# Row maxima of an attention block taken over every sixth query, and carried to their row by one transfer

## The chip, the cores and the metric

The kernel runs on one core of a Trainium2 chip. The metric is the device time of one execution in microseconds (us), the median of several. Matrix products run on TensorE (PE in the rows, with PEld for the loading of its weights), reductions on VectorE (DVE), exponentials and copies on ScalarE (ACT), some additions on GpSimd (POOL), and nearly all transfers are issued by SyncE (SP).

## The reference

Attention over 2 x 8 heads of 768 queries and keys with 64 values each, in which a query sees only the keys of its own cluster, and then two MLPs on the 1536 tokens. What the change touches is the maximum of each query's scores:

```
mask = q_assign[:, :, :, None] == k_assign[:, :, None, :]
scores = scale * np.matmul(q, k.transpose(0, 1, 3, 2))
scores = np.where(mask, scores, -1000000000.0)
scores = scores - np.max(scores, axis=-1, keepdims=True)
attn = np.exp(scores)
attn = attn / (np.sum(attn, axis=-1, keepdims=True) + 1e-09)
return np.matmul(attn, v).astype(np.float32)
```

## The kernel before

The 16 heads (h = 0 to 15) go one after the other through a software pipeline whose order is written out by hand, engine by engine. After it come the MLPs, whose order is set by a planner; the change doesn't touch them.

For each head, two tensors of 128 partitions hold what the products need: `q2(h)` and `k2(h)`, each with two layers of 768 columns. In layer 1, rows 0 to 63 are the queries (keys), rows 64 to 79 mark the cluster, and row 96 (`MROW`) of `q2` holds, for each of the 768 queries, the negative of its maximum. `k2` has ones in that row, so that the scores come out of TensorE with the maximum taken off.

The scores (`st`, line 707) are made with keys on the partitions: 12 steps per head (6 blocks of 128 keys by 2 halves of 384 queries), each of two matmuls: the first over layer 0, the second over rows 0 to 96 of layer 1, `MROW` among them. Beside each step of head h, one of the 12 matmuls `smax` (line 657) of head h + 1 runs: a block of 128 queries is the weight (80 rows by 128 columns), 384 keys are streamed, and VectorE takes the maximum of each query's 384 scores into `nm[:, c, n]` (line 662).

After the 12 steps, `mneg(h + 1)` (line 673) reduces the two halves to `nr`, 128 partitions by 6 numbers, with the sign turned. Block c holds the queries c*128 to c*128 + 127, so partition p of `nr` has the queries p, 128 + p, 256 + p and so on. To bring them into one row in order, `mrow` multiplies `nr` by the identity on TensorE (out: 6 partitions by 128), ScalarE copies the result from PSUM to `row`, and one transfer on SP sends its 6 pieces of 512 bytes to `MROW`. In the heads 2 to 14 the two products with the values of blocks 0 and 1 (`values(h, 0)`, `values(h, 1)`, line 739: `pv`) stand ahead of `mrow` on TensorE, and the rest of the values (`pv`, and the sums `ps`) behind it. The odd heads 5 to 11 have eight more matmuls (`sims`, line 572) between the last step and the values. Head 1 calls `mrow(2)` in another place, ahead of products of another kind (line 807). In all, `mrow` runs 14 times. The heads 0 and 1 get their maxima in another way (`mrow_at_once`), which stays.

The first matmul of head h + 1 that reads `MROW` is the second `st` of its first step, after all values of head h. The first `smax` beside it, of head h + 2, reads rows of `k2` that ScalarE has cast (line 642) in the even heads.

Of the kernel before, what the change touches and what calls it, by code (L numbers as in the profile page):

```python
# [8 lines left out]
F32 = mybir.dt.float32  # L9
F32R = mybir.dt.float32r  # L10
# [174 lines left out]
def tile_cluster_attention_two_mlps(ctx: ExitStack, tc: tile.TileContext, qk, v, cen, w1, w2, wg, wv, w3, out):  # L185
    nc = tc.nc
    B, H, D, _, S = qk.shape
    NC = cen.shape[0] // H
# [4 lines left out]
    SC = S // 128  # L193
# [26 lines left out]
    def take_bank(pl, tag, shape, name):  # L220

        if tag == "m":
            bank[0] ^= 1
            tag = f"m{bank[0]}"
        return pl.tile(shape, F32, tag=tag, name=name)
# [168 lines left out]
    sm_p = pool(att, "sm", 2)  # L394
    r_p.append(pool(att, "r1", 1))
    ps_x = pool(att, "ps_x", 1, space=PSUM)
# [20 lines left out]
    ONE, MROW = D, 96  # L417

    def q2(h):
        return q2_t[h % NQK]  # L420
# [140 lines left out]
    ident_r = acst.tile([128, 128], F32R, name="ident_r")  # L561

    def similar(hs, pl=ps_x, tag="x"):


        out = []
        for h in hs:
            ps = take_bank(pl, tag, [128, 512], "sims")[:, 0:HALF]
            todo = [(i, n) for i in (0, 1) for n in range(2)]
            for at, (i, n) in enumerate(todo):  # L570
                o = LEAD + 128 * (h % H) - 32 * (2 * n + i)
                nc.tensor.matmul(  # L572
                    out=ps,
                    lhsT=cs[:, i, o:o + 128],
                    rhs=(q2, k2)[i](h)[:, 0, n * HALF:(n + 1) * HALF],
                    start=(at == 0),
                    stop=(at == len(todo) - 1),
                )
            out.append(ps)
        return out  # L580
# [71 lines left out]
    def smax(h, c, n, pl, tag):  # L652

        if c == 0 and n == 0:
            nm_t[h] = sm_p.tile([128, SC, 2], F32, tag="nm", name="nm")
        ps = take_bank(pl, tag, [128, 512], "smax")[:, 0:HALF]
        nc.tensor.matmul(  # L657
            out=ps,
            lhsT=q2(h)[0:ONE + NC, 1, c * 128:(c + 1) * 128],
            rhs=k2(h)[0:ONE + NC, 1, n * HALF:(n + 1) * HALF],  # L660
        )
        nc.vector.tensor_reduce(out=nm_t[h][:, c, n:n + 1], in_=ps, axis=AX.X, op=ALU.max)  # L662
# [5 lines left out]
    nr_t = {}  # L668

    def mneg(h, cs=slice(None)):  # L670
        if h not in nr_t:
            nr_t[h] = sm_p.tile([128, SC], F32R, tag="nr", name="nr")
        nc.vector.tensor_reduce(out=nr_t[h][:, cs], in_=nm_t[h][:, cs, :], axis=AX.X, op=ALU.max, negate=True)
# [9 lines left out]
            )  # L683
        nc.scalar.copy(q2(h)[MROW:MROW + 1, 1, n * HALF:(n + 1) * HALF], ps)

    def mrow(h, pl=ps_x, tag="x"):

        ps = take_bank(pl, tag, [SC, 128], "mrow")
        nc.tensor.matmul(out=ps, lhsT=nr_t.pop(h), rhs=ident_r)  # L689
        row = sm_p.tile([SC, 128], F32R, tag="row", name="row")  # L690
        nc.scalar.copy(row, ps)
        nc.sync.dma_start(
            out=q2(h)[MROW:MROW + 1, 1, :].rearrange("p (c s) -> p c s", s=128).bitcast(F32), in_=row.bitcast(F32)
        )

    p_t = {}
# [307 lines left out]
    for h in range(NH):  # L1004
        more, ahead = h + 1 < NH, h + 4 < NH
        maxima = list(steps) if more and h > 1 else []
        for i, step in () if h in (0, NH - 1) else list(enumerate(steps))[2 * EARLY if h == 1 else 0:]:
            scores(h, *step)
            if maxima:
                next_smax(h + 1, maxima)  # L1010
            if h > 1:
                beside_scores(h, i)
            if h > 2 and i == 4:
                moved_sums(h - 1)
                send_sums(h - 1)
        if h == NH - 1:
            moved_sums(h - 1)
            send_sums(h - 1)
            load_sums((h - 3) // 2)
        elif h > 2:  # L1020
            moved(h - 1)
            if h % 2 and 4 < h < NH - 1:
                load_sums((h - 3) // 2)
        if h == 0:
            load_qk(5)
        if h == 1:
            do(assign([2, 3], (nc.vector.tensor_copy, nc.gpsimd.tensor_copy)))
            norm(0)
            lo_k(4, nc.gpsimd)
            lo_q(4, nc.gpsimd)  # L1030
        if h == 2:
            norm(1)
        if 1 < h < NH - 1:
            mneg(h + 1)
            if h % 2 and ahead and h > 3:
                do(largest([h + 3, h + 4], similar([h + 3, h + 4], ps_s, "s")))
            if h > 3 and h + 5 < NH:
                hi_staged(h + 5)
            values(h, 0)
            values(h, 1)  # L1040
            mrow(h + 1)
        casts = [] if not h else [h + 4] if h < 3 else [7, 8] if h == 3 else [h + 5] if h + 5 < NH else []
        if h > 3 and casts:
            hi_others(casts[0])
        elif casts and h != 1:
            hi_q(casts[0])
            hi_k(casts[0])
        elif casts:
            hi_q(casts[0])
        if h % 2 == 0 and 0 < h < NH - 3:  # L1050
            do(assign([h + 2, h + 3]))
        if NH - 4 <= h < NH - 1:
            close_slot(h % NQK)
        if h == NH - 4:
            w_p = right("w", WB - 1)
        if h == NH - 3:
            s_p.append(right("s", 1))
            b_p.update({i: right(f"b{i}", 1) for i in (1, 2)})
        if h == NH - 2:
            b_p[0] = right("b0", 1)  # L1060
            c_p.append(right("c", CB // 2))
            e_p.append(right("e", 1))
        for c in range(SC) if more else ():
            if h > 1:
                if c > 1:
                    values(h, c)
                beside_block(h, c)
            elif h or c:
                pv(h, c)
            if c == 0:  # L1070
                if h < 2:
                    load_v(h + 1)
                    if h:
                        load_v(h + 2)
                        hi_k(casts[0])
                    for i in casts:
                        lo_q(i, nc.gpsimd)
                        lo_k(i, nc.gpsimd)
                    load_qk(h + 6)
                if ahead:  # L1080
                    if h + 5 == NH:
                        close_slot(FIRST)
                        close_slot("st")
                        xs_p.append(right("xs", 2))
                        xc_p.append(right("xc1", XC - X0 - 1))
            if h == 0:
                beside(1, c, ((ps_m, "m"), (ps_s, "s")))
                if c == 2:
                    sims = similar([2])
                if c == 3:  # L1090
                    mneg(1)
                    mrow_at_once(1, 0, ps_o, "o")
                    mrow_at_once(1, 1, ps_m, "m")
                    sims += similar([3], ps_m, "m")
                    do(largest([2, 3], sims))
                if c in (3, 4):
                    for step in steps[EARLY * (c - 3):EARLY * (c - 2)]:
                        scores(1, *step)
            if h == 1:
                beside(2, c, ((ps_m, "m"), (ps_s, "s")))  # L1100
                if c == 3:
                    mneg(2)
                    sims = similar([4], ps_s, "s")
                    mrow(2)
                if c == 4:
                    do(largest([4, 5], sims + similar([5], ps_s, "s")))
            for i in casts[-1:] if h > 3 else ():
                for at, step in ((1, lo_staged), (2, spread_lo)):
                    if c == at:
                        step(i)  # L1110
            if h > 1 and c == 2:
                if h + 2 < NH:
                    load_v(h + 2)
                if h + 6 < NH:
                    load_qk(h + 6)
            for part in takes.get((h, c), ()):
                take(part)
            if h in (2, 3) and c == 1:
                lo_q(casts[0])
                lo_k(casts[0])  # L1120
            for n in beside_values.get((h, c), ()):
                next(more_steps[n], None)
            if h == 1 and c == 4:
                fetch_to(2)
            if h == 3 and c == 4:
                do(largest([6, 7], similar([6, 7], ps_s, "s")))
                hi_staged(8)
                hi_others(8)
            if h == 4 and c == 1:
                lo_staged(8)  # L1130
                spread_lo(8)
            if h == 3 and c in (3, 4):
                to_x(0, c - 3)
# [568 lines left out]
```

## Time and profile before

| | |
|---|---|
| median of 3 runs | 776.87 us (776.78 to 777.65) |
| profiled execution, own time | 778.64 us |
| its span | 776.9 us |
| TensorE busy in the span | 769.1 us (99%) |
| VectorE, ScalarE, GpSimd busy | 665.6, 504.6, 126.6 us |
| chain that ended last, TensorE's share | 92% |
| `mrow` matmuls (line 689) | 14 |
| `smax` matmuls (line 657), heads 0 to 15 | 192 |

A span is the time from the first to the last instruction of the profiled execution; 1.7 us lie around it. The busy time of TensorE is partly modelled, so that a busy TensorE can still lose time between two matmuls. The chain of work that ended last shows this better: it is followed back from the last instruction and gives each piece the time until the next one.

### The profile page before, as it was taken

The numbers are of one execution on the slowest core, as the hardware profiler recorded it, in microseconds if no ns is written. First come the engines' busy times: TensorE is split into PE (matmuls) and PEld (weight loads), VectorE is DVE, ScalarE is ACT, GpSimd is POOL, SyncE is SP. The second block draws the span as 40 slices with busy tenths as digits, with TensorE's granted clock in tenths as the row PEclk, the third lists the DMA queues.
The fourth block names the chain that finished last, engine by engine and source line by source line (L and its number), as shares of the span: only waits on it lengthen the run. The fifth ranks groups of instructions, "written<-read, shape, count | busy, mean of one in ns | idle before, by whom it ended". The sixth has DMA issues, their size and how long they took to land.

```text
span 776.9 us, 11963 instructions
## 1 busy us (share of the span) xinstructions
PE 769.1 (99%) x4238; PEld 662.6 (85%) x4238; DVE 665.6 (86%) x1220; ACT 504.6 (65%) x875; POOL 126.6 (16%) x136
## 2 busy tenths in 40 slices
PE   8999999999999999999999999999999999999998
PEld 6996676766767999999999999999999999999996
DVE  7887899998994999999798889999987997877752
ACT  7848988996866877777676677666544644443322
POOL 7655344453544000100000000000000000000000
PEclk9999999999999999999999999999999999999999
DMA  4231155643214686653186783657433122412102
GB/s 114 51 101 37 37 137 146 171 105 80 65 33 157 220 268 208 211 176 105 39 271 225 279 282 109 232 173 234 136 109 107 57 82 82 135 56 82 55 1 81
DMA packets 52507, 101.94 MB, mean 131 GB/s; under 512 B 19600, under 2 KB 25088, under 8 KB 52448
## 3 DMA queue, kind: packets, MB, share of 16 engines
q1 hardware_dynamic: 52224, 100.86, 41.5%
q8 instruction: 33, 0.54, 0.3%
q10 hardware_dynamic: 224, 0.33, 0.1%
q14 instruction: 26, 0.21, 0.1%
HBM read 76.23 MB, written 21.06 MB: 125 GB/s over the span
## 4 chain that ended last, share of the span: by engine, by line
PE 92%; DVE 5%; ACT 1%; issue 1%; POOL 1%; DMA 0%; POOLq 0%; DVEq 0%; ACTq 0%
PE h L384 36%; PE a L384 29%; PE st L707 8%; PE pv L739 7%; PE smax L657 4%; PE ps L739 3%; PE pv L807 2%; PE sims L572 2%; DVE nm L662 1%; PE warm L492 1%; DVE b L379 0%; DMA w<-scr 0%; DVE u L1301 0%; PE mrow L689 0%; DVE wo L291 0%
## 5 line engine op out<-in xcount | busy, mean ns | idle before, releaser
L384 PE MATMUL h<-xc,b 128*128 128x384 f32 x1680 | 317.0, 337 | 0.1
L384 PEld LDWEIGHTS h<-xc,b 128*128 128x128 f32 x1680 | 291.5, 188 | 10.6 <-DVE u L1301 2.4
L384 PE MATMUL a<-g,sp 128*128 128x512 f32 (+1 forms) x768 | 144.3, 337 | 0.0
L384 PEld LDWEIGHTS a<-g,sp 128*128 128x128 f32 x768 | 125.0, 188 | 16.8
L384 PE MATMUL a<-sp,g 128*128 128x512 f32 x432 | 109.6, 393 | 0.0
L726 POOL TENSOR_TENSOR add<-p 128x384 f32<-128x384 f32 x84 | 84.4, 1026 | 105.4 <-ACT p L717 104.4
L662 DVE TENSOR_REDUCE nm<-smax 128x1 f32<-128x384 f32 x192 | 97.6, 553 | 4.5 <-PE smax L657 4.0
L717 ACT ACTIVATE p<-st 128x384 f32<-128x384 f32 x192 | 87.9, 491 | 20.6 <-PE st L707 15.7
L707 PE MATMUL st<-q,k 128*128 128x384 f32 (+1 forms) x384 | 97.8, 345 | 0.1
L384 PEld LDWEIGHTS a<-sp,g 128*128 128x128 f32 x432 | 80.2, 188 | 13.2
L376 ACT CAST b<-s 128x512 fp32r<-128x512 f32 x80 | 49.5, 619 | 56.0 <-PE h L384 45.5
L707 PEld LDWEIGHTS st<-q,k 128*128 128x128 f32 (+1 forms) x384 | 68.2, 190 | 10.0 <-issue 7.2
L739 PE MATMUL pv<-p,v 128*64 128x384 f32 x336 | 65.2, 495 | 0.0
L657 PE MATMUL smax<-k,q 80*128 80x384 f32 x192 | 63.5, 348 | 1.1 <-DVE nm L662 0.9
L1301 DVE TENSOR_TENSOR u<-h,p 128x384 f32<-128x384 f32 x80 | 44.1, 552 | 21.9 <-PE h L384 21.6
L280 ACT ACTIVATE a<-raw 128x512 f32<-128x512 f32 x68 | 45.5, 670 | 19.5 <-issue 9.4
L379 DVE TENSOR_TENSOR b<-s,b 128x512 fp32r<-128x512 f32 x80 | 54.6, 684 | 1.6 <-ACT b L376 0.4
L379 DVE TENSOR_TENSOR g<-c,g 128x768 fp32r<-128x768 f32 x56 | 52.5, 951 | 1.6 <-ACT g L376 0.9
L376 ACT CAST g<-c 128x768 fp32r<-128x768 f32 x56 | 45.3, 835 | 12.3 <-DVE c L1316 11.8
L286 DVE SCALAR_TENSOR_TENSOR t<-a,t 128x512 int32<-128x512 int32 x68 | 46.0, 682 | 4.0 <-ACT t L283 4.0
L1309 ACT ACTIVATE c<-c 128x384 f32<-128x384 f32 (+1 forms) x56 | 38.3, 684 | 16.8 <-DVE c L1301 16.1
L376 ACT CAST b<-w 128x768 fp32r<-128x768 f32 x35 | 29.2, 834 | 29.2 <-PE h L384 28.8
(144 smaller groups left out, 904.6 us busy)
## 6 DMA issues: line engine op xcount, KB each, us to landing
raw<-in_w SPq DMA_DIRECT2D x44, 512.0 KB
w<-scr SPq DMA_DIRECT2D x30, 512.0 KB
raw<-in_wg SPq DMA_DIRECT2D x12, 512.0 KB
raw<-in_wv SPq DMA_DIRECT2D x12, 512.0 KB
w<-scrg SPq DMA_DIRECT2D x12, 512.0 KB
w<-scrv SPq DMA_DIRECT2D x12, 512.0 KB
st<-in_qk SPq DMA_DIRECT2D x31, 192.0 KB
scr<-wd SPq DMA_DIRECT2D x23, 256.0 KB
```

What stands on the lines that cost most here:

```text
L280: nc.scalar.activation(a, raw[:, :, 1].bitcast(F32), ACTF.Copy, scale=2.0**-112)
L286: nc.vector.scalar_tensor_tensor(out=t, in0=a.bitcast(I32), scalar=3, in1=t, op0=ALU.logical_shift_left, op1=ALU.bitwise_or)
L376: nc.scalar.copy(to, of)
L379: eng.tensor_tensor(out=to, in0=of, in1=hi.bitcast(F32), op=ALU.subtract)
L384: nc.tensor.matmul(out=out_ps, lhsT=lhs[a], rhs=rhs[b], start=(start and j == 0), stop=(stop and j == 2), skip_group_check=True, **kw)
L657: nc.tensor.matmul(out=ps, lhsT=q2(h)[0:ONE + NC, 1, c * 128:(c + 1) * 128], rhs=k2(h)[0:ONE + NC, 1, n * HALF:(n + 1) * HALF],)
L662: nc.vector.tensor_reduce(out=nm_t[h][:, c, n:n + 1], in_=ps, axis=AX.X, op=ALU.max)
L707: nc.tensor.matmul(out=ps, lhsT=k2(h)[0:rows, a, c * 128:(c + 1) * 128], rhs=q2(h)[0:rows, a, at], start=(a == 0), stop=(a == 1),)
L717: nc.scalar.activation(p_t[h, c][:, n * HALF:(n + 1) * HALF], ps, ACTF.Exp, scale=scale)
L726: nc.gpsimd.tensor_tensor(out=add_t[h, c][:, at], in0=p_t[h, c][:, at], in1=p_t[h, c + 1][:, at], op=ALU.add)
L739: nc.tensor.matmul(out=ps[n * D:(n + 1) * D, 0:HALF], lhsT=w, rhs=x[:, n * HALF:(n + 1) * HALF], start=start, stop=stop, skip_group_check= ...
L1301: lambda: nc.vector.tensor_tensor(out=to.tile[:, part], in0=ps.tile[:, 0:HALF], in1=other.tile, op=ALU.add),
```

## The change

In the heads 2 to 15, block c of `smax` takes the queries c, c + 6, c + 12 and so on (`c::SC`, SC is 6): the 128 columns of the weight then lie 24 bytes apart, where they were side by side. Partition p of `nr` so holds the six queries 6p to 6p + 5, which are neighbours in `MROW`. The matmul by the identity, the copy from PSUM and the tile `row` are gone; `mrow` is one transfer from `nr` itself, 128 pieces of 24 bytes. The call of `mrow` moves up behind `mneg`.

```
@@ smax
-            lhsT=q2(h)[0:ONE + NC, 1, c * 128:(c + 1) * 128],
+            lhsT=q2(h)[0:ONE + NC, 1, c::SC] if h > 1 else q2(h)[0:ONE + NC, 1, c * 128:(c + 1) * 128],
@@ mrow
-    def mrow(h, pl=ps_x, tag="x"):
-
-        ps = take_bank(pl, tag, [SC, 128], "mrow")
-        nc.tensor.matmul(out=ps, lhsT=nr_t.pop(h), rhs=ident_r)
-        row = sm_p.tile([SC, 128], F32R, tag="row", name="row")
-        nc.scalar.copy(row, ps)
+    def mrow(h):
+
         nc.sync.dma_start(
-            out=q2(h)[MROW:MROW + 1, 1, :].rearrange("p (c s) -> p c s", s=128).bitcast(F32), in_=row.bitcast(F32)
+            out=q2(h)[MROW:MROW + 1, 1, :].rearrange("i (p c) -> i p c", c=SC).bitcast(F32), in_=nr_t.pop(h).bitcast(F32)
         )
@@ the loop over heads
             mneg(h + 1)
+            mrow(h + 1)
...
             values(h, 0)
             values(h, 1)
-            mrow(h + 1)
@@ head 1
                     mneg(2)
+                    mrow(2)
                     sims = similar([4], ps_s, "s")
-                    mrow(2)
```

The instructions of TensorE in head 6, from the last `smax` of the steps to the sums (`pv` and `ps` are the products with the values and with ones; `x4` counts equal instructions in a row). Before:

```order
L657 MATMUL smax<-k_2_181,q_2_180 128x384
L739 MATMUL pv<-p,v_190 64x384 x4
L689 MATMUL mrow<-ident_r,nr 6x128
L739 MATMUL pv<-p,v_190 64x384 x2
L739 MATMUL ps<-add,ones 64x384 x2
L739 MATMUL pv<-p,v_190 64x384 x2
```

The same place with the change:

```order
L735 MATMUL pv<-p,v_190 64x384 x6
L735 MATMUL ps<-add,ones 64x384 x2
L735 MATMUL pv<-p,v_190 64x384 x2
L735 MATMUL ps<-add,ones 64x384 x2
L735 MATMUL pv<-p,v_190 64x384 x4
```

Six `pv` now follow each other where `mrow` stood between the fourth and the fifth. Nothing else on TensorE moves, here or in the other heads.

SP in head 6, from the sums that it sends out to the loads of the cast rows (`q_2` and `q_1` are the `q2` of two heads, `oT` the cluster rows, `st` the staged queries and keys). Before:

```order
L772 DMA sums<-sums 2x384
L692 DMA q_2_180<-row 1x6x128
L644 DMA q_4_170<-oT 16x768
L644 DMA k_4_171<-oT 16x768
L793 DMA r<-recips 64x768 x2
```

With the change:

```order
L768 DMA sums<-sums 2x384
L688 DMA q_2_180<-nr 1x128x6
L644 DMA q_4_170<-oT 16x768
L644 DMA k_4_171<-oT 16x768
L789 DMA r<-recips 64x768 x2
```

The transfer keeps its place among SP's; it now reads `nr` and so waits for VectorE, where it waited for ScalarE's copy.

## Rows read from the trace of the kernel before

**Rows 1.** Busy time by stage, head 6 and two of the MLPs; x counts instructions.
```profile
core 0: us, PE busy (x) PEld busy (x) DVE busy (x) ACT busy (x) POOL busy (x), PEclk, DMA share, GB/s
...
110.60:123.40 12.80, 12.80 (x75) 8.81 (x73) 11.62 (x24) 12.06 (x23) 5.94 (x6) 1.00 0.67 187
...
250.00:400.00 150.00, 149.98 (x852) 139.06 (x851) 140.78 (x245) 110.61 (x189) 2.21 (x1) 1.00 0.55 179
400.00:600.00 200.00, 199.94 (x1104) 186.27 (x1103) 182.97 (x327) 125.02 (x207) 0.00 (x0) 1.00 0.57 192
```

**Rows 2.** Chain that ended last, head 6: start, length until the next piece.
```profile
117.24 1.44 PE pv L739 x8
118.68 0.15 PE mrow L689
118.83 0.80 PE pv L739 x4
...
121.56 1.29 PE pv L739 x8
```

**Rows 3.** The same chain, head 5.
```profile
105.85 0.16 PE mrow L689
106.00 0.80 PE pv L739 x4
```

**Rows 4.** Timeline, ScalarE and weight loads, end of head 10; in brackets idle time and releaser.
```profile
173.95 0.25 ACT L691 CAST row<-mrow 6x128 fp32r<-6x128 f32 x1
...
177.61 0.83 ACT L642 CAST k<-oT 16x768 fp32r<-16x768 f32 x1
...
178.49 0.19 PEld L657 LDWEIGHTS smax<-k,q 80*128 80x128 f32 x1 [0.26 <-ACT k L642]
```

**Rows 5.** Timeline, `mrow` of head 2; chain, `mrow` of head 1.
```profile
62.26 0.22 PE L689 MATMUL mrow<-ident_r,nr 128*6 128x128 f32 x1 [0.17 <-DVE nr L673]
...
50.30 0.06 PE mrow L689
```

**Rows 6.** Chain in head 5's steps, then in an MLP; the last row is the latter's timeline.
```profile
100.19 0.18 PE smax L657
100.37 0.35 PE st L707 x2
...
394.94 0.59 PE a L384 x5
...
394.78 0.75 PE L384 MATMUL a<-g,sp 128*128 128x256 f32 x5
```

**Rows 7.** Groups by line: operation, tiles, shapes, count, busy us, mean ns, idle before.
```profile
L657 PEld LDWEIGHTS smax<-k,q 80*128 80x128 f32 x192 | 35.8, 190 | 4.5 <-DVE nm L662 2.3 <-ACT k L642 1.4 <-POOL k L634 0.5
L739 PEld LDWEIGHTS pv<-p,v 128*64 128x64 f32 x336 | 21.5, 136 | 24.3 <-issue 20.7 <-PE st L707 2.5 <-ACT k L444 0.2
```

**Rows 8.** Two VectorE lines: duration min/median/max in ns, first and last start.
```profile
L603 DVE TENSOR_REDUCE T<-U x14: 560/565/569, 34.0 to 188.1; 128x192 f32<-128x384 f32 x14
...
L608 DVE TENSOR_REDUCE mx<-T x9: 352/553/554, 10.9 to 188.7; 128x24 f32<-128x384 f32 x7, 128x12 f32<-128x192 f32 x2
```

**Rows 9.** Timeline around one carrying of the maxima, head 6.
```profile
117.87 0.17 DVE L673 TENSOR_REDUCE nr<-nm 128x6 fp32r<-128x12 f32 x1
...
119.73 0.77 SPq L692 DMA_DIRECT2D q<-row  x1
...
123.43 0.30 PEld L707 LDWEIGHTS st<-q,k 128*128 128x128 f32 x2 [0.60 <-issue]
```

**Rows 10.** Timeline, transfers of 128 pieces of 48 bytes, and what waited for them.
```profile
232.89 0.34 SPq L780 DMA_DIRECT2D rc<-sums  x1
...
234.54 1.03 DVE L784 TENSOR_SCALAR rc<-rc 128x12 f32<-128x12 f32 x1 [2.96 <-DMA rc<-sums]
...
301.51 0.47 SPq L788 DMA_DIRECT2D recips<-rc  x1
...
305.89 1.11 SPq L793 DMA_DIRECT2D r<-recips  x2
```

## The prediction

> **What bounds the kernel now.** I read the busy times by stage first. In head 6, which has no `sims`, TensorE is busy for all of the 12.80 us, in the MLPs for 149.98 of 150 us and 199.94 of 200 us, at a granted clock of 1.00 throughout [rows 1]. So TensorE bounds nearly every stage, and what it is spared in the heads should reach the end: the MLPs have no TensorE wait worth the name in which it could be lost. VectorE is the next (11.62 us of head 6), ScalarE with 12.06 us close beside it [rows 1]. But busy TensorE is not TensorE at its peak, so I read the chain of work that ended last next, since it gives each piece the time until the next one starts. There the reader is to see that a piece of four `pv` records costs 0.65 us in a plain run (eight take 1.29), but 0.80 us right behind `mrow` [rows 2].
>
> **The change part by part.**
>
> *The product by the identity, removed.* In the chain, `mrow` takes 0.15 us in head 6 and 0.16 in head 5, and the four `pv` behind it 0.80 us in both [rows 2, 3], where half of a plain eight would take 0.645. So a `mrow` costs 0.155 us for itself and 0.155 us for the start of another kind of product behind it, 0.31 us in all. The first `pv` of a head pay such a start too (1.44 us for eight instead of 1.29, [rows 2]); that one stays. The heads 2 to 14 have 13 of these: 13 x 0.31 = 4.03 us. Head 1's stands ahead of products of another kind and costs 0.06 us [rows 5]. In head 2 TensorE also stood for 0.17 us until `nr` was there [rows 5]; that wait goes. Sum so far: 4.03 + 0.06 + 0.17 = 4.26 us, all on TensorE's path.
>
> *The copy from PSUM, removed.* 14 copies of 0.25 us on ScalarE. It stands on the path in one place: in the even heads ScalarE works without a gap from the last exponential to the cast of `k` (line 642), on which the first `smax` of the next head waits 0.26 us [rows 4]. There TensorE comes 0.31 us earlier, but ScalarE only 0.25 plus the 0.03 us between two instructions, 0.28. In up to five such places 0.03 us of the gain stay behind: -0.15 us. What comes late next there is the same cast, no new wait.
>
> *The transfer.* It has the same place in SP's queue, between the sums and the cluster rows, and waits for VectorE's `nr` instead of ScalarE's copy, which came later in any case; so nothing queued behind it (the transfers of `oT`, then `recips`) waits longer. In head 6 `nr` is done at 118.04, SP issued at 119.73, and the head ends at 123.43, where the next head's first `st` starts; the second reads the row [rows 9]. Issued at about 118.1, the new transfer has 123.43 + 0.18 - 0.31 - 118.1 = 5.2 us; in the heads with `sims` 1.4 us more. No row shows 128 pieces of 24 bytes that land in a single partition. The nearest are 128 pieces of 48 bytes: a reader of one waited until 1.65 us after its issue, and another had to wait 4.38 us [rows 10]. Both are shorter than 5.2, so I take nothing for it; this cover has 0.8 us to spare at the slow end.
>
> The Trainium skill, page "DMA: Bandwidth & Descriptors", section Specifications, gives 512 bytes as the least size at line rate and says that smaller ones are read, modified and written. By that the new pieces are of the slow sort where the old ones, at 512 bytes, were not; the rows on 48 bytes are of the slow sort too, and the sum by it would be the same as long as they land in time.
>
> *The weights, 24 bytes apart.* 14 heads x 12 = 168 loads of `smax` now read columns with a step. No row of TensorE shows such a load, so I bound it. Three matmuls of a step follow each other at 0.53 us, 0.177 each [rows 6]. Loads of 128 columns can come faster than that: matmuls of 256 columns with weights of the same size pass every 0.59 / 5 = 0.118 us [rows 6]. So a load has 0.059 us of room behind the stream of 384 columns, and is free until it takes half as long again. The lower bound is therefore nothing; a gain is excluded, because no byte less is read. For the upper bound: a load of 128 columns takes 190 ns, one of 64 takes 136 [rows 7], so 128 columns are 108 ns of reading. If each took twice as long, a load would need 118 + 108 = 226 ns, 49 more than the 177 that it has: 168 x 0.049 = 8.2 us. The nearest row is VectorE's: the reduction on line 603 reads SBUF in steps of 64 bytes, two far places in turn, and takes 565 ns for 384 numbers; line 608 reads as many side by side in 553 [rows 8]. That is 12 ns per 384, some 4 ns per 128. I go by this row and take zero, with 8.2 us kept for the range.
>
> **Sum.** 4.26 - 0.15 = 4.1 us less, which I round to 4.0. The profiled execution took 778.64 us with a span of 776.9 and would take 774.6; the median of the runs, 1.8 us below it, goes from 776.87 to 772.9.
>
> **The rivals.**
>
> *Loads at half rate.* Each column is then a fetch of its own, a load outlasts the stream, and TensorE waits in all 168 places: +8.2 - 4.0 = 4.2 us slower, 781.1; with the room taken as exact and no overhead (216 instead of 226 ns), +6.5 - 4.0 = 779.4. It decides against the change once a load takes 177 + 4000 / 168 = 201 ns. For it speaks that TensorE reads a column in 0.84 ns, faster than VectorE's 1.4; against it the 12 ns of [rows 8], though those two places are each revisited for neighbouring numbers.
>
> This is what a rule of the Trainium skill would make of it: the page "SBUF — State Buffer", section "Door 1: The DMA port swizzle", has lines of 16 bytes, wants two hits on a line for full bandwidth, and lets fp32 step by four at most. A step of six never hits a line twice. The VectorE row doesn't bear that out for its engine; no row tells of TensorE.
>
> *Loads in between.* At 180 to 200 ns per load the gain is mostly eaten: 773.4 to 776.8.
>
> *The transfer lands late.* If 128 writes to one partition take longer than the 5.2 us, the second `st` of a head waits, and everything behind it on TensorE. One microsecond too late in the seven even heads costs 7 us, 779.9. Against it speak both rows of 48 bytes.
>
> *The time is gained and given back.* The MLPs could wait for weights that don't come earlier. Against it: 0.08 us of waits in 350 us [rows 1].
>
> **How the numbers follow.** Forecast, 772.3 to 774.7: 0.59. Loads in between, or a gain given back: 0.14, of which 0.04 still faster than 775.3. Half rate: 0.19. A late transfer, or loads far slower than half rate: 0.08. About 0.2%, 1.6 us, is what can be told from no change here. So faster 0.63, same 0.10, slower 0.27. Likeliest 772.9, its own range 772.2 to 774.7. For 8 in 10 the range must reach into the half-rate case, whose own span is 779.4 to 781.1; it ends at 781.0.
>
> **What would show it.** The chain in head 6 should have twelve `pv` in 1.44 + 0.65 us without a break, and the head should last 12.5 us instead of 12.83. The piece `smax` with its two `st` should stay at 0.53 us; if it reads 0.57 to 0.58, the loads are at half rate, and the group of `smax` loads should then show some 300 ns instead of 190. If a wait of `st` for a transfer `q<-nr` appears at the start of a head, the transfer is late. I am wrong if the steps lengthen by more than 0.024 us each, or if TensorE's idle time in the MLPs grows by microseconds.

## The result, and the profile after

The changed kernel takes 782.07 us in the median of six runs (781.97 to 783.19), the kernel before 776.87: a ratio of 1.0062, with a 95% interval from 1.0051 to 1.0073. It is slower by 4.0 to 5.7 us, where 4.0 us less had been forecast, and lies 1.1 us above the end of the range.

The profiled execution of before reached the products with the values of head 0 some 1.1 us later than the one after (24.58 against 23.45 us below), ahead of anything that the change touches, so the two spans, 776.9 and 780.3 us, don't give the difference. I measure from a fixed place instead: from the first twelve products with the values in head 0 to the scores of head 15, behind which the MLPs begin. Chain that ended last, before:

```profile
24.58 1.29 PE pv L807 x12
...
231.63 2.52 PE st L707 x12
```

After:

```profile
23.45 1.29 PE pv L803 x12
...
234.88 2.52 PE st L703 x12
```

That is 207.05 us before and 211.43 after, 4.38 us more. (Each such figure comes from one execution; the runs give the interval.) From there to the end of the span it is 545.27 and 545.42 us: the MLPs neither lost nor gave back anything. The chain after, in head 6, answers to [rows 2] and to the step of [rows 6]:

```profile
112.25 0.36 PE st L703 x2
...
114.94 0.22 PE smax L657
115.17 0.36 PE st L703 x2
...
118.08 2.09 PE pv L735 x12
```

Two things are to be seen. The twelve `pv` take 2.09 us without a break, where `mrow` and the two pieces around it took 1.44 + 0.15 + 0.80 = 2.39: the gain of 0.30 us is there. But a step of three matmuls takes 0.58 us, where it took 0.53. Ten steps lie between 112.25 and 118.08, 0.583 us each. In head 6 before, eleven lie between this row and the first `pv` at 117.24 [rows 2], 0.532 each:

```profile
111.39 0.36 PE st L707 x2
```

So a step is some 51 ns longer. The loads of the weights show why; the row answers to the first of [rows 7] (duration min/median/max in ns; the 24 loads of heads 0 and 1 have no step in their columns and give the minimum):

```profile
L657 PEld LDWEIGHTS smax<-k,q x192: 186/305/329, 13.0 to 228.4; 80*128 80x128 f32 x192
```

305 ns instead of 190. Both, the longer step and the longer load, are the signs that the prediction had named for loads at half rate. The transfer that answers to [rows 9] was no trouble:

```profile
L688 SPq DMA_DIRECT2D q<-nr x14: 494/526/544, 49.5 to 229.7; - x14
...
DMA to landing us min/median/max: 2.0/2.0/2.6
```

It was issued in 0.53 us instead of 0.77, and its 128 pieces landed after 2.0 us, 2.6 at most; no `st` waits for it. The busy times by stage answer to [rows 1]:

```profile
110.80:124.00 13.20, 13.20 (x75) 9.54 (x73) 11.38 (x21) 11.54 (x21) 5.94 (x6) 1.00 0.62 180
...
400.00:600.00 200.00, 199.95 (x1105) 186.15 (x1104) 183.10 (x325) 126.54 (x208) 0.00 (x0) 1.00 0.57 195
```

TensorE is busy without a gap at a granted clock of 1.00, as before. The busy share doesn't tell the two kernels apart; only the chain and the loads do.

### The profile page after: what moved, and what is told of

It is laid out like the page before. It is cut to its first block, busy times and chain, and to the rows that moved or that the text cites. A ratio compares the mean times of both kernels' runs of the same rounds, so it can differ in the third digit from the quotient of the medians.

```text
span 780.3 us, 11927 instructions
## 1 busy us (share of the span) xinstructions
PE 773.4 (99%) x4224; PEld 672.1 (86%) x4224; DVE 668.7 (86%) x1220; ACT 504.4 (65%) x861; POOL 126.5 (16%) x136
## 4 chain that ended last, share of the span: by engine, by line
PE 93%; DVE 5%; ACT 1%; issue 1%; DVEq 0%; ACTq 0%
PE h L384 36%; PE a L384 29%; PE st L703 9%; PE pv L735 7%; PE smax L657 5%; PE ps L735 3%; PE pv L803 2%; PE sims L572 1%; DVE nm L662 1%; DVE b L379 1%; PE warm L492 0%; DVE s L1241 0%; DVE u L1297 0%; DVE wo L291 0%; DVE g L379 0%
## 5 line engine op out<-in xcount | busy, mean ns | idle before, releaser
L713 ACT ACTIVATE p<-st 128x384 f32<-128x384 f32 x192 | 90.5, 492 | 33.0 <-PE st L703 26.6
L662 DVE TENSOR_REDUCE nm<-smax 128x1 f32<-128x384 f32 x192 | 102.5, 555 | 8.0 <-PE smax L657 5.0
L703 PEld LDWEIGHTS st<-q,k 128*128 128x128 f32 (+1 forms) x384 | 70.6, 196 | 10.0 <-issue 7.2
L657 PE MATMUL smax<-k,q 80*128 80x384 f32 x192 | 72.3, 394 | 0.7 <-DVE nm L662 0.2
L735 PE MATMUL pv<-p,v 128*64 128x384 f32 x336 | 62.4, 491 | 0.0
L657 PEld LDWEIGHTS smax<-k,q 80*128 80x128 f32 x192 | 54.8, 292 | 4.0 <-DVE nm L662 1.8
```

What stands on the lines that cost most here:

```text
L657: nc.tensor.matmul(out=ps, lhsT=q2(h)[0:ONE + NC, 1, c::SC] if h > 1 else q2(h)[0:ONE + NC, 1, c * 128:(c + 1) * 128], rhs=k2(h)[0:ONE + N ...
L703: nc.tensor.matmul(out=ps, lhsT=k2(h)[0:rows, a, c * 128:(c + 1) * 128], rhs=q2(h)[0:rows, a, at], start=(a == 0), stop=(a == 1),)
L713: nc.scalar.activation(p_t[h, c][:, n * HALF:(n + 1) * HALF], ps, ACTF.Exp, scale=scale)
L735: nc.tensor.matmul(out=ps[n * D:(n + 1) * D, 0:HALF], lhsT=w, rhs=x[:, n * HALF:(n + 1) * HALF], start=start, stop=stop, skip_group_check= ...
```

## The experiments

Each ratio below is against runs of the kernel before that were made beside the experiment; their medians were 777.49 and 777.32 us.

### The transfer without the step in the weights

```
-            lhsT=q2(h)[0:ONE + NC, 1, c::SC] if h > 1 else q2(h)[0:ONE + NC, 1, c * 128:(c + 1) * 128],
+            lhsT=q2(h)[0:ONE + NC, 1, c * 128:(c + 1) * 128],
```

> The changed kernel with one part undone: the queries of a block lie side by side again for the weights of smax, as before the change; the maxima still go to their row by one transfer of 128 pieces of 24 bytes, with no product by the identity. Left out: the order of the maxima, so each query has another query's maximum taken off. Theory A, the loss of the change is the loading of smax's weights with a step and nothing else: the loads read 190 ns again, three matmuls of a step take 0.53 us, twelve pv of a head 2.09 us, and the time is 776.87 - 4.1 = 772.8 us (772.0 to 773.6). Rival B, the small transfers into one partition slow TensorE or the steps: the steps stay at 0.57 to 0.59 us though the loads read 190 ns, and the time is 777 us or more.

Measured: 773.95 us, ratio 0.9954 (0.9940 to 0.9967), 2.6 to 4.7 us less than before. The loads are back at 190 ns and a step at 0.53 us:

```profile
L657 PEld LDWEIGHTS smax<-k,q x192: 186/190/192, 14.2 to 221.0; 80*128 80x128 f32 x192
```

So the small transfers don't slow TensorE, and rival B falls. By the ratio the time is 773.3 us, within theory A's range. Of the 4.1 us of the forecast's gain, the runs show 3.6.

### The step in the weights without the transfer

The opposite edit, in the kernel before:

```
-            lhsT=q2(h)[0:ONE + NC, 1, c * 128:(c + 1) * 128],
+            lhsT=q2(h)[0:ONE + NC, 1, c::SC] if h > 1 else q2(h)[0:ONE + NC, 1, c * 128:(c + 1) * 128],
```

> The kernel before with one part of the change alone: smax takes every sixth query as its weights from head 2 on, while the product by the identity, the copy from PSUM and the transfer of 6 pieces of 512 bytes stay. Left out: the order of the maxima. Theory A: loads of smax read about 305 ns, each of the 168 steps takes 0.586 us instead of 0.53, and the time is 776.87 + 168 x 0.056 = 786.3 us (785.3 to 787.3). Rival B: the loads are long in the record but the steps keep 0.53 to 0.55 us, and the time is 776.9 to 780.

Measured: 785.87 us, ratio 1.0108 (1.0094 to 1.0122), 7.3 to 9.5 us more. Theory A's 168 x 0.056 = 9.4 is near the end of that interval, and rival B falls. In the chain:

```profile
23.26 1.29 PE pv L807 x12
...
239.01 2.53 PE st L707 x12
```

215.75 us, 8.70 more than before, or 0.052 us for each of the 168 loads. The two parts together, by the ratios, make -3.6 + 8.4 = +4.8 us, and the change itself showed +4.4 in its chain and +4.0 to +5.7 in its runs: nothing else is needed to explain the loss.

### The load against the distance of the columns

```
+    STEP = {2: 1, 3: 1, 4: 2, 5: 3, 6: 4, 7: 5, 8: 6, 9: 4, 10: 3, 11: 2, 12: 1, 13: 6, 14: 5, 15: 2}
...
-            lhsT=q2(h)[0:ONE + NC, 1, c::SC] if h > 1 else q2(h)[0:ONE + NC, 1, c * 128:(c + 1) * 128],
+            lhsT=q2(h)[0:ONE + NC, 1, 0:128 * STEP[h]:STEP[h]] if h > 1 else q2(h)[0:ONE + NC, 1, c * 128:(c + 1) * 128],
```

> The changed kernel, with another distance between the columns of smax's weights in each head: 1 in heads 2, 3 and 12, 2 in heads 4, 11 and 15, 3 in heads 5 and 10, 4 in heads 6 and 9, 5 in heads 7 and 14, 6 in heads 8 and 13 (in fp32 numbers). Left out: which queries a block takes, so that the maxima are not theirs. It gives the load time against the distance in one trace. Theory A1, a cost that begins where a column no longer shares 16 bytes with its neighbour: 190 ns for 1 to 3 or 4, about 305 ns for 5 and 6. Theory A2, a cost in proportion to the bytes passed over: 190 at 1, 213 at 2, 236 at 3, 259 at 4, 282 at 5, 305 at 6. Theory A3, any distance over 1 costs the same: 305 ns from 2 on.

This kernel ran once, for its trace. The loads of `smax` alone, by stretch (us; then their busy time and count, the granted clock, the transfers). The stretches are the steps of heads 3, 4, 5, 6, 7, 8, 9, 10 and 11, whose `smax` belong to the next head, with distances of 2, 3, 4, 5, 6, 4, 3, 2 and 1 numbers:

```profile
65.00:71.80 6.80, 2.35 (x12) 1.00 0.41 99
80.00:87.50 7.50, 3.03 (x12) 1.00 0.00 0
93.00:101.10 8.10, 3.74 (x12) 1.00 0.77 176
108.00:115.70 7.70, 3.65 (x12) 1.00 0.90 253
121.00:129.10 8.10, 3.66 (x12) 1.00 0.92 198
136.00:143.70 7.70, 3.69 (x12) 1.00 0.86 227
149.00:156.50 7.50, 3.03 (x12) 1.00 0.82 187
163.00:171.00 8.00, 2.37 (x12) 1.00 0.61 158
176.00:183.90 7.90, 2.28 (x12) 1.00 0.75 167
```

Divided by twelve: 190 ns side by side, 196 to 198 at 2, 252 at 3, 308 to 312 at 4, 304 at 5, 305 at 6. None of the three theories fits as it was written: A1 had 3 for free, A2 had 6 dearer than 4, A3 had 2 at full price. What does fit is a price for each new line of 16 bytes that the columns touch: 128 columns touch 32 lines side by side, 64 at a distance of 2, 96 at 3 and 128 from 4 on. From 2 to 3 and from 3 to 4 the 32 more lines cost some 55 and 58 ns, about 1.75 ns each. From 32 to 64 lines only 6 to 8 ns are added; there the columns themselves, at 0.84 ns each, seem to be the limit. The load doesn't care how busy the transfers are: the two stretches at a distance of 3 have DMA shares of 0.00 and 0.82 and the same 3.03 us.

The Trainium skill, page "SBUF — State Buffer", section "Door 1: The DMA port swizzle", names lines of 16 bytes, of which two hits are wanted for full bandwidth; this trace agrees, since a distance of 2 with two numbers on a line is all but free (196 ns), while one number on a line adds 115 ns, as much again as the estimated 108 ns of reading. The same paragraph lets fp32 step by four for free; here a distance of four takes 308 to 312 ns, as much as six, so the measurement decides against that half.

### Two numbers on a line

```
-            lhsT=q2(h)[0:ONE + NC, 1, c::SC] if h > 1 else q2(h)[0:ONE + NC, 1, c * 128:(c + 1) * 128],
+            lhsT=q2(h)[0:ONE + NC, 1, c // 2 * 256 + c % 2:(c // 2 + 1) * 256:2] if h > 1 else q2(h)[0:ONE + NC, 1, c * 128:(c + 1) * 128],
...
+        nr = nr_t.pop(h)
+        for g in range(SC // 2):
+            nc.sync.dma_start(
+                out=q2(h)[MROW:MROW + 1, 1, g * 256:(g + 1) * 256].rearrange("i (p c) -> i p c", c=2).bitcast(F32),
+                in_=nr[:, g * 2:(g + 1) * 2].bitcast(F32),
+            )
```

> The changed kernel with blocks of every second query within 256 queries, so that the columns of smax's weights lie 8 bytes apart; the maxima go to their row in three transfers of 128 pieces of 8 bytes. It computes the reference. Theory A1 (a cost only where a column no longer shares 16 bytes with its neighbour): loads of 190 ns, steps of 0.53 us, 772.8 us (772.0 to 774). Theory A2 (in proportion to the bytes passed over): loads of 213 ns, which the 59 ns of room hide, and the same 772.8 us. Theory A3 (any distance): loads of 305 ns and 782 us, as the changed kernel. If the three transfers land too late at the end of a head, the first st of the next head waits for them by name and up to 13 us are added.

Measured: 774.03 us, ratio 0.9955 (0.9942 to 0.9967): faster than both kernels. The loads take 196 ns in the median. In the chain:

```profile
23.34 1.28 PE pv L806 x12
...
42.16 0.77 PE smax L657 x4
...
226.43 2.52 PE st L706 x12
```

203.09 us, 3.96 less than before; the four `smax` in a row belong to the next experiment. From 226.43 to the end of the span of 771.7 us it is 545.27 us, as in the kernel before: the MLPs give nothing of the gain back. The three transfers land after 2.0 us each in the median, 3.4 at most, and no `st` waits for one.

### Three numbers on 16 bytes and a bit

The same with 3 in place of 2 and two transfers.

> As step_two, with every third query within 384: columns 12 bytes apart, two transfers of 128 pieces of 12 bytes. It computes the reference. steps_by_head had loads of 3.03 / 12 = 0.252 us at this distance, 62 ns more than 190. Theory A with the room of 59 ns between two matmuls of 384 columns: 3 ns of each load come through, 168 x 0.003 = 0.5 us, so 773.4 us, against 772.8 without (ratio 0.9955 as transfer_only and step_two, 0.994 to 0.9975). Rival C, there is no such room and a longer load is paid in full: 168 x 0.062 = 10.4 us, 783 us.

Measured: 775.27 us, ratio 0.9971 (0.9961 to 0.9982). Rival C falls; the room is real. It is 1.2 us behind `step_two`, where 0.5 was expected. In the chain:

```profile
23.43 1.29 PE pv L806 x12
...
42.25 0.84 PE smax L657 x4
...
227.97 2.51 PE st L706 x12
```

204.54 us, 1.45 more than in `step_two`. The 12 loads of head 2 stand four in a row without `st` between them, and there is less to hide them; but the three fours take 0.84, 0.82 and 0.82 us where `step_two` has 0.77, 0.76 and 0.76, which is 0.19 us in all. The rest, 1.26 us, is 8 ns for each of the other 156 loads, where 3 had been expected; why they slow by 5 ns more than the room allows is open.

### Single numbers in six transfers

Blocks of neighbouring queries, as before the change, and six transfers of 128 pieces of 4 bytes.

> The changed kernel with the blocks of 128 neighbouring queries of the kernel before; the maxima go to their row in six transfers of 128 pieces of 4 bytes, one after the other on SP. It computes the reference. The loads read 190 ns. SP needs six issues of some 0.5 us, so the last transfer is issued 2.6 us after the first and lands 2.0 us later, some 4.7 us after nr is done, where 5.2 us are there in the even heads. Theory A: 772.8 us, as transfer_only, with a ratio near 0.9955. Rival D, the transfers land late: the first matmuls st of a head wait for them by name, each microsecond too late costs up to 7 us in the even heads, and the ratio is 1.000 or more.

Measured: 775.89 us, ratio 0.9981 (0.9971 to 0.9991). The ratio lies between theory A's 0.9955 and the 1.000 of rival D: more than half of the gain is lost, 2.0 us against `step_two`. Rival D's wait is there, by name (waits of TensorE: us in all, times, longest):

```profile
PE st L706 <- DMA q<-nr: 2.1, 3, 0.9
```

Three heads wait up to 0.9 us, 2.1 us in all, which is about the loss. So the end of a head holds one to three small transfers, and six are too many. The rival "the transfer lands late" was a real one, though not for the change as it was made.

### Do other readers pay for single numbers too?

> step_two with extra work at the end of head 6, read by nobody: for the distances 1, 2, 3, 4 and 6 (fp32 numbers), two reductions on VectorE and two copies on ScalarE of 128 numbers per partition, and eight matmuls with 32 weights that stream 128 columns. Theory E1, the cost of a distance belongs to SBUF and meets every reader: from 4 on VectorE and ScalarE take some 100 ns longer, and so does a matmul. Theory E2, only TensorE's loading of weights shows it: VectorE and ScalarE take the same at all distances within 10 ns, as line 603 did, and the matmuls pass at one pace. Theory E3, it is a pace of reading lines of 1.75 ns: engines that take a number in 1 ns lose 0.7 ns per number from 4 on, 90 ns per instruction, and the stream of a matmul, which takes a column in 0.42 ns, loses already at 2.

This kernel and the next ran once each, for their traces. Two reductions on VectorE and two copies on ScalarE of 128 numbers, at distances of 1, 2, 3, 4 and 6, each row the pair (timeline: start, us):

```profile
124.96 0.60 DVE L993 TENSOR_REDUCE pr<-q 128x1 f32<-128x128 f32 x2 [3.72 <-DMA q<-st]
125.65 0.63 ACT L995 COPY pr<-q 128x128 f32<-128x128 f32 x2 [5.03 <-DVE pr L993]
126.62 0.61 DVE L993 TENSOR_REDUCE pr<-q 128x1 f32<-128x128 f32 x2
127.32 0.64 ACT L995 COPY pr<-q 128x128 f32<-128x128 f32 x2 [1.04 <-DVE pr L993]
128.30 0.68 DVE L993 TENSOR_REDUCE pr<-q 128x1 f32<-128x128 f32 x2
129.07 0.76 ACT L995 COPY pr<-q 128x128 f32<-128x128 f32 x2 [1.12 <-DVE pr L993]
130.17 0.81 DVE L993 TENSOR_REDUCE pr<-q 128x1 f32<-128x128 f32 x2
131.07 0.86 ACT L995 COPY pr<-q 128x128 f32<-128x128 f32 x2 [1.25 <-DVE pr L993]
132.28 0.81 DVE L993 TENSOR_REDUCE pr<-q 128x1 f32<-128x128 f32 x2
133.18 0.88 ACT L995 COPY pr<-q 128x128 f32<-128x128 f32 x2 [1.24 <-DVE pr L993]
```

The eight matmuls at the distances 1 and 6:

```profile
125.08 1.03 PE L998 MATMUL pr<-q 128*32 128x128 f32 x8 [4.92 <-DMA q<-st]
132.31 1.09 PE L998 MATMUL pr<-q 128*32 128x128 f32 x8 [0.98 <-DVE pr L999]
```

E2 falls: from 4 on, VectorE takes 105 ns longer per reduction and ScalarE 115 to 125 per copy; a distance of 2 is all but free and 3 lies between, as for the weights. VectorE does pay, then, though line 603 had not shown it. For these two engines E1 (some 100 ns) and E3 (90) are too close to be told apart. For the matmuls E1 fails: it had some 100 ns for each from 4 on, 0.8 us for eight, and they take 1.03 us at a distance of 1 and 1.09 at 6. (They ran at a granted clock of 0.50, the lower of its two levels, 1.2 GHz, after TensorE had waited 4.92 us; what a stream pays at full clock shows in the next run.)

### Why line 603 had not shown it

> step_two with extra work at the end of head 6, read by nobody: VectorE and ScalarE copy 128 numbers per partition, twice each, from four patterns of places, in this order: side by side; pairs of neighbours 24 bytes apart; two places 64 bytes apart in turn, each of which moves on by one number (the pattern of line 603, on which the prediction rested); single numbers 24 bytes apart. TensorE streams, eight times each, 384 columns side by side, 384 columns 8 bytes apart, 128 side by side and 128 columns 24 bytes apart, over 128 weights. Theory F1, what costs is a fetch that brings one number, and a place once fetched is kept while another is read: the first three patterns take the same within 10 ns, the fourth some 110 ns longer (probe_steps: 430 instead of 315 ns on ScalarE); line 603 told nothing of single numbers. Theory F2, only the last place is kept: the third pattern costs as much as the fourth. Theory F3, it is the distance between neighbours in the order of reading: the second pattern already costs half of it. For the stream of a matmul: G1, it pays as the other readers do, so that 384 columns 8 bytes apart stay at 0.177 us but 128 columns 24 bytes apart go from 0.11 to 0.22 us; G2, it doesn't pay at either.

ScalarE, in the order side by side, pairs 24 bytes apart, two places in turn (the pattern of line 603), singles 24 bytes apart; each row is a pair of copies:

```profile
125.64 0.63 ACT L1001 COPY pr<-q 128x128 f32<-128x128 f32 x2 [4.91 <-DVE pr L999]
...
128.76 0.65 ACT L1001 COPY pr<-q 128x128 f32<-128x128 f32 x2 [2.50 <-DVE pr L999]
...
132.35 0.68 ACT L1001 COPY pr<-q 128x128 f32<-128x128 f32 x2 [2.94 <-DVE pr L999]
...
134.07 0.89 ACT L1001 COPY pr<-q 128x128 f32<-128x128 f32 x2 [1.04 <-DVE pr L999]
```

315, 325, 340 and 445 ns per copy. VectorE's copies take 0.49 us per pair in the first three and 0.59 in the fourth:

```profile
131.77 0.49 DVE L999 COPY pr<-q 128x128 f32<-128x128 f32 x2
...
133.40 0.59 DVE L999 COPY pr<-q 128x128 f32<-128x128 f32 x2
```

F1 holds in kind, with 25 ns on ScalarE in place of 10 for two places in turn, and 50 ns instead of 110 for VectorE's single numbers: a copy pays half of what a reduction paid. That a place is kept while another is read, so that the jumps to and fro of line 603 touch few new lines, fits this; nothing else was tried for it. F2 falls, and F3 too, for pairs 24 bytes apart cost 10 ns.

For the stream of a matmul both G1 and G2 fall as written. Three stretches of these matmuls alone (us; then their busy time and count, the granted clock, the transfers) hold 384 columns 8 bytes apart, 128 side by side and 128 columns 24 bytes apart, all at a granted clock of 1.00:

```profile
129.00:131.40 2.40, 2.34 (x7) 1.00 0.00 0
131.70:133.00 1.30, 1.11 (x8) 1.00 0.00 0
133.40:134.90 1.50, 1.17 (x8) 1.00 0.04 11
```

The first kind again, the last five and the last four of the eight (timeline: start, us):

```profile
129.46 1.88 PE L1005 MATMUL pr<-q 128*128 128x384 f32 x5
129.80 1.54 PE L1005 MATMUL pr<-q 128*128 128x384 f32 x4
```

At 8 bytes one matmul of 384 columns starts 0.34 us after the other, where the steps of [rows 6] have 0.177 side by side: a stream pays nearly double at a distance that costs a weight load next to nothing. At 24 bytes eight matmuls of 128 columns take 1.17 us against 1.11, so there a column takes at most 1.17 / 8 / 128, or 1.1 ns, and the 1.75 ns of the weight loads is not the price of a stream.

## Why the prediction was wrong

**The forecast that failed is the step on the weights: "I go by this row and take zero."** The upper bound beside it was the right value. It had 8.2 us for loads of twice the reading time; `step_only` lost 8.4 us by its ratio and 8.70 in its chain. Per load it had 108 ns more, and 115 was measured; per step 49 ns, and 51 to 52 was measured.

**Why the row misled.** Line 603 was the nearest strided read in the trace, but what it has in common with the new loads is the distance, and distance is not what costs. The sentence on the rival had seen the difference ("those two places are each revisited for neighbouring numbers") and still gave half rate a chance of 0.19. Two probes bear the objection out for the engine of that row: VectorE pays 105 ns for a reduction of 128 single numbers and 50 for a copy of them, and nothing that shows for two places in turn.

**The rule and the row.** The prediction set the rule of two hits on a line, from the Trainium skill, page "SBUF — State Buffer", section "Door 1: The DMA port swizzle", beside the half-rate rival and gave the row of line 603 more weight. The loads of 305 ns agree with the rule.

**The gain was right, its sum in part by luck.** 0.31 us per `mrow` was forecast, 0.30 shows in head 6, and 4.1 us in all: 3.6 by the ratio of `transfer_only`, 3.96 in the chain of `step_two`. Both halves of the cost were there, the product and the second start of `pv` behind it. But between the first `st` of one head and of the next, `step_two` is 0.6 us shorter than the kernel before in head 3, twice the forecast, and 0.1 us longer in head 13. There TensorE, now earlier, waits for an exponential of ScalarE, for which the sum had no term:

```profile
202.93 0.62 PE L706 MATMUL st<-q,k 128*128 128x384 f32 x2 [0.17 <-ACT p L716]
```

**The room was about right.** It was put at 59 ns between two matmuls of 384 columns. Loads 62 ns longer made a step 8 ns longer where the room leaves 3, and loads 115 ns longer made it 51 to 52 ns longer where it leaves 56.

**The transfer was right in kind.** No cost was taken, and no `st` waited; it landed in 2.0 us, near the quicker of the two rows of 48 bytes (1.65 us), and in 2.6 at most; in `transfer_only` the slowest took 3.8, nearer to the slower row (4.38) and still inside the 5.2 us of cover. The cover gave out only when six transfers stood in a row.

**Nothing given back in the MLPs, right.** 545.27 us in `step_two`, which has the gain, and 545.27 in the kernel before.

**The range** ended at 781.0, inside the half-rate case's own span, to leave out no more than two in ten. That case came, and came 1.0 us above its upper value of 781.1: the gain was 3.6 us by its ratio instead of 4.0, and the loss 8.4 instead of 8.2; the rest is within the interval of the runs.

## What to carry to other kernels

In these runs, weights read with a step were all but free at a distance of two fp32 numbers, where two of them share 16 bytes. They were dearer by half of the reading time at three, and cost the full double from four on; whether that matters is decided by the room that the stream of the matmul beside them leaves, which two rows of the trace give (here 0.177 us per matmul against 0.118 for the shortest with the same load). A regrouping that serves a transfer can often be had in smaller groups: pairs gave the whole gain here, with three transfers for one. The operand that is streamed is another matter: it cost nearly double already at a distance of two. And a nearest row must agree with the new operation in what the price hangs on, in this case how many new lines are touched, not how far apart they are.

## What the runs showed of the hardware that was not expected

By the fit above, a new line of 16 bytes cost a weight load 1.75 ns (55 and 58 ns for 32 more of them), whether the next number lay 16, 20 or 24 bytes off. A stream of 384 columns paid at 8 bytes already, 0.34 us instead of 0.177 at a granted clock of 1.00. VectorE's reductions and ScalarE's copies paid much the same per 128 single numbers, 105 and 115 to 125 ns, VectorE's copies 50; two places in turn cost ScalarE 25 ns and VectorE nothing that shows. A transfer of 128 pieces of 24, 8 or 4 bytes into one partition landed in 2.0 us in the median of `after`, `step_two` and `by_words`, and in 2.2 in `transfer_only`.
